# Block transposes of ten head pairs on VectorE: placed later, in quarters, each pair hashed by itself, value means per pair

## The chip, the cores and the metric

The kernel runs on one core of a Trainium2 chip. The metric is the device time of one execution in microseconds (us); lower is better. The engines are TensorE (PE in the profile; PEld is its weight loads), VectorE (DVE), ScalarE (ACT), GpSimd (POOL) and the queues that issue DMAs, above all SyncE's (SP). Each engine works through its own instructions in order; between engines there are semaphores.

## The reference

Attention in which a query sees only the keys of its own hash bucket, followed by a gated feed-forward block on the normalised result (4 batches, 8 heads, 768 tokens, 64 columns per head):

```python
    q_bits = (np.einsum('bhsd,dk->bhsk', q, proj) > 0).astype(np.int64)
...
    mask = q_bucket[:, :, :, None] == k_bucket[:, :, None, :]
    scores = np.where(mask, scale * np.matmul(q, k.transpose(0, 1, 3, 2)), -1000000000.0)
    attn = np.exp(scores - np.max(scores, axis=-1, keepdims=True))
    attn = attn / (np.sum(attn, axis=-1, keepdims=True) + 1e-09)
    x = np.matmul(attn, v)
...
    xn = x / np.sqrt(np.mean(x * x, axis=-1, keepdims=True) + 1e-06) * rms_g
    g = xn @ w_gate
    out = (g * (1.0 / (1.0 + np.exp(-g))) * (xn @ w_val)) @ w_out
```

## The kernel before, in words

**Units, slots and stages.** The work is cut into eight units u: half the queries (384) of a batch b = u // 2. A unit has eight heads, and a head three chunks of keys; so there are 192 chunks. The main loop at the end of the function has one *slot* t for each of them. In slot t the program issues the score matmuls of chunk t + 1 (`scores`, L337), the Exp of chunk t (`probs`, L349, on ACT), and then whatever the list `plan[t]` holds. The n-th Exp in the trace therefore marks slot n. 24 slots are a *stage*: stage w has slots 24w to 24w + 23. `at(w, s, f, ...)` puts a step into slot 24w + s, and steps of one slot are issued in the order in which they were put there.

**Regular steps.** `av` (L362) multiplies the probabilities of a head by the values, in two parts, into `o_ps`, of which there is one buffer for a pair of heads. After the second head of a pair comes `attn_out`: VectorE adds the mean of the values (`otmp`, L376, which reads `o_ps` and `cvb`), takes the reciprocal (L381), and POOL makes `x` (L383) and its square `sq` (L388). `sumsq` (L392, VectorE) sums the square some slots later. In slot 4 of stages 2 to 7 stands `norm` of the unit just finished: `ss` on VectorE (L402), `rstd` on POOL (L406), then three `xn` on VectorE (L409). Around slots 5 to 7 `turn_x` turns `xn` on TensorE (`x_ps`, L416) and VectorE writes it back (`xnT`, L422). Then `gate` and `value` run the feed-forward's first two products (L433): ACT takes a tanh (L441), VectorE makes `a` (L450) and `ht` (L451). `project` (L462) does the last product of the unit before, and `store` copies it out on ACT (L474) and sends it through SP (L475).

**Banks.** `d_ps` (hash), `m_ps` (value mean), `x_ps`, `g_ps`, `v_ps` and `y_ps` share three PSUM banks: a tile takes a bank that is free in program order and waits on the chip until its previous tenant has been read.

**Placing.** `spread` puts the 36 project matmuls, the turns of x and the 96 feed matmuls of a stage into its 24 slots by weights (in ns), so that each slot gets an equal share. The dictionary `hashes` (slot: weight, step) takes part in this: a hash takes its place ahead of a whole piece in its slot, and its weight pushes later pieces back.

**Pairs of heads.** q and k of a pair (b, hp) must be turned so that the 64 columns lie on partitions. Six pairs, (0, 0) to (0, 3), (1, 0) and (1, 1), are turned on TensorE. The other ten are loaded in blocks of 32 columns (`load_blocks`, L117, eight DMAs on SP; `load_v`, L103) and turned on VectorE (`turn_dve`, a 32x32 block transpose: L175 for batch 1, L181 for batches 2 and 3), k and q in two halves each. POOL casts the turned tiles to fp16 into `QK` (`cast_pool`, L194), and the values into `vl` (`v_prep`, L305); for batches 2 and 3 it also adds up values (`v_sum`, L311 to L313). `v_mean` (L321) sums values over the tokens on TensorE with a matrix of ones, and VectorE writes `cvb` (L324).

**Hashes.** `hash_one` multiplies k and q of a pair by the projection (L202, four matmuls into four row groups of one bank), takes signs (L210), spreads them into two head forms (`select`, L217, two instructions) and sends them by four DMAs on SP (L278) into rows 64 to 75 of `QK`, where `scores` reads them. `hash_two` does two pairs at once in two banks, with two sign instructions, two selects of double width and four DMAs (L297).

**Where things stand before.** The dictionary `spots` gives for each batch the slots of the loads and of the first half turn; the four halves go into four consecutive slots. Pairs (1, 2) and (1, 3) are hashed by `hash_one` in slots 52 and 60, the other eight by `hash_two` in slots 80, 93, 111 and 135. The block transposes end in slot 132.

Of the kernel before, what the change touches and what calls it, by code (L numbers as in the profile page):

```python
# [9 lines left out]
FP16 = mybir.dt.float16  # L10
# [6 lines left out]
S = 768  # L17
# [4 lines left out]
HALF = 384  # L22
# [9 lines left out]
def kernel(  # L32
# [12 lines left out]
    nc = tc.nc  # L45
# [10 lines left out]
    spool = ctx.enter_context(tc.tile_pool(name="spool", bufs=2))  # L56
# [24 lines left out]
    def bank(name, shape=None, dt=FP32):  # L81
        return gps.tile(shape or [128, 512], dt, name=name, tag="g")
# [47 lines left out]
    ONPE = [(0, hp) for hp in range(4)] + [(1, 0), (1, 1)]  # L130
    KROWS = D + 12
    KROWS0 = D + 6
    qT, kT, QK = {}, {}, {}
# [34 lines left out]
            turned(b, hp, which)[64 * e : 64 * e + 64, h0 : h0 + n, :],  # L168
        )

    def turn_dve(b, hp, which, part):
        src = raw[b, hp][0 if which == "q" else 1]
        dst = (qT if which == "q" else kT)[b, hp]
        if b in PARITY:
            nc.vector.transpose(  # L175
                dst.rearrange("p (e j t r) -> p e r j t", e=2, j=3, r=4)[:, part],
                src.rearrange("p (r j e) d -> p e r j d", j=3, e=2)[:, part],
            )
            return
        r = slice(2 * part, 2 * part + 2)  # L180
        nc.vector.transpose(  # L181
            dst.rearrange("p (c t r) -> p r c t", c=6, r=4)[:, r],
            src.rearrange("p (r c) d -> p r c d", r=4)[:, r],
        )
# [13 lines left out]
    def hash_half(parts):  # L198

        ps = bank("d_ps", [128, HALF])  # L200
        for t, src in parts:
            nc.tensor.matmul(  # L202
                ps[32 * t : 32 * t + 32, :], pj[:, 0:32], src,
                start=True, stop=True, tile_position=(0, 32 * t),
            )
        return ps

    def signs(bt, ps, c0, n):

        nc.vector.tensor_scalar(  # L210
            out=bt[0:n, 1, c0 : c0 + HALF], in0=ps[0:n], scalar1=0.0, scalar2=0.5,
            op0=ALU.is_gt, op1=ALU.subtract,
        )

    def select(bt, n, w):
        for hh in range(2):
            nc.vector.tensor_scalar_mul(  # L217
                bt[0:n, hh, 0:w], bt[0:n, 1, 0:w], sel[0:n, hh : hh + 1]
            )
# [15 lines left out]
    def hash_direct(b, hp, heads):  # L235


        where = [(which, hh) for which in "kq" for hh in heads]
        pss = hash_pairs([turned(b, hp, which)[:, hh, :] for which, hh in where])
        bt = spool.tile([128, 2, S], FP16, name="bits")  # L240

        def sign(e):
            signs(bt[:, :, e * HALF :], pss[e], 0, 32 * len(where))

        def move(e, kinds="kq", n=1, only=heads):
            for t, (which, hh) in enumerate(where):
                if which in kinds and hh in only:
                    o = (0 if which == "q" else S) + e * HALF
                    nc.vector.tensor_scalar_mul(
                        QK[b, 2 * hp + hh, "h"][64:KROWS0, o : o + n * HALF],  # L250
                        bt[32 * t : 32 * t + 6, 1, e * HALF : (e + n) * HALF],
                        4.0 * BIT * BIT if which == "k" else 1.0,
                    )

        def send():
            nc.vector.tensor_scalar_mul(bt[:, 0, :], bt[:, 1, :], own)
            for t, (which, hh) in enumerate(where):
                o = 0 if which == "q" else S
                nc.sync.dma_start(
                    out=QK[b, 2 * hp + hh, "h"][64:KROWS0, o : o + S],  # L260
                    in_=bt[32 * t : 32 * t + 6, 0, :],
                )

        return sign, move, send

    def hash_one(b, hp):
# [9 lines left out]
        for t, which, half in where:  # L276
# [2 lines left out]
                out=QK[b, hp][64:KROWS, :, o : o + HALF],  # L279
                in_=bt[32 * t : 32 * t + 12, :, 0:HALF],  # L280
            )

    def hash_two(b, hp):

        bt = spool.tile([128, 2, S], FP16, name="bits")
        for half in range(2):
            c0 = half * HALF
            ps = hash_half(
                [(2 * i + j, t[b, hp + i][:, c0 : c0 + HALF])
                 for i in range(2) for j, t in enumerate((kT, qT))]  # L290
            )
            signs(bt, ps, c0, 128)
        select(bt, 128, S)
        for i in range(2):
            for j, o in enumerate((S, 0)):
                p0 = 64 * i + 32 * j
                nc.sync.dma_start(  # L297
                    out=QK[b, hp + i][64:KROWS, :, o : o + S], in_=bt[p0 : p0 + 12]
                )


    def v_prep(b, hp):
# [204 lines left out]
    for t in range(4):  # L507
        p0 = 32 * t
# [36 lines left out]
    NS = 24  # L545
# [5 lines left out]
    def at(w, s, f, *a):  # L551
        plan[NS * w + s].append(lambda: f(*a))
# [7 lines left out]
    sign, move, _ = hash_direct(0, 0, (0,))  # L560
# [63 lines left out]
    for hp, ts in ((0, (8, 22, 23, 24, 25, 24, 26, 26, 28, 42)), (1, (12, 27, 28, 29, 30, 29, 41, 32, 33, 43))):  # L624
        tl, ts = ts[0], ts[1:]
        for w in "kq":
            at(0, tl, load_natural, nc.sync, 1, hp, w)
        at(0, tl, load_v, nc.sync, 1, hp)
        at(0, ts[0], new_pair, 1, hp)
        for t, hh, w in zip(ts[0:4], (0, 1, 0, 1), "kkqq"):  # L630
            at(0, t, turn_pe, 1, hp, hh, w)
        at(0, ts[4], cast_pool, 1, hp, "k")
        at(0, ts[5], cast_pool, 1, hp, "q")
        at(0, ts[6], hash_pair, 1, hp)
        at(0, ts[7], send_pair, 1, hp)
        at(0, ts[8], v_prep, 1, hp)
        at(2, 6 + 6 * hp, v_mean, 1, hp, 2, range(6))
    spots = {
# [3 lines left out]
    }  # L642
    sqs = {}

# [19 lines left out]

    SCORES, AV, PROJ, FEED, TURN = 330, 290, 216, 324, 220
    hashes = {t: (700, hash_one, 1, hp) for hp, t in ((2, 52), (3, 60))}
    for b, ts in ((2, (80, 93)), (3, (111, 135))):
        for i, t in enumerate(ts):  # L670
            hashes[t] = (1430, hash_two, b, 2 * i)

    def spread(t0, n, pieces):
        fixed = [SCORES + (AV if (t - 1) % 3 < 2 else 0) for t in range(t0, t0 + n)]
# [22 lines left out]
    for u in range(7):  # L697
# [11 lines left out]
        for i in range(9):  # L709
            c, n = divmod(i, 3)  # L710
# [9 lines left out]
    for t, (_, *step) in hashes.items():  # L720
        at(0, t, *step)

    for b, (loads, turns) in spots.items():
        for hp in range(4):
            if (b, hp) in ONPE:
                continue
            t = loads[hp]
            at(0, t, load_blocks, nc.sync, b, hp)
            at(0, t, load_v, nc.sync, b, hp)
            t = turns[hp]  # L730

            late = 5 if t % NS == 0 else 0
            at(0, t, new_pair, b, hp)
            at(0, t, turn_dve, b, hp, "k", 0)
            at(0, t + 1, turn_dve, b, hp, "k", 1)
            at(0, t + 2 + late, cast_pool, b, hp, "k")
            at(0, t + 2, turn_dve, b, hp, "q", 0)
            at(0, t + 3, turn_dve, b, hp, "q", 1)
            at(0, t + 4 + late, cast_pool, b, hp, "q")
            at(0, t + 5 + late, v_prep, b, hp)  # L740
            if b > 1:
                at(0, t + 5 + late, v_sum, b, hp)
                if hp % 2:
                    at(2 * b, 1 + hp, v_mean, b, hp - 1, 4)
            else:
                at(2 * b, 6 + 6 * hp, v_mean, b, hp, 2, range(6))


    def head_of(t):
# [61 lines left out]
```

## Time and profile before

| | us |
|---|---|
| three runs | 347.31, 347.76, 347.92; median 347.76 |
| the profiled execution | 348.43 |
| its span in the trace | 346.7 |

| engine | busy us | share of the span | instructions |
|---|---|---|---|
| PE | 330.3 | 95% | 3031 |
| DVE | 246.5 | 71% | 477 |
| ACT | 225.9 | 65% | 327 |
| POOL | 147.4 | 43% | 210 |

| group | line | count | mean ns |
|---|---|---|---|
| block transposes of k / q, batches 2 and 3 | L181 | 16 / 16 | 881 / 873 |
| block transposes of k / q, batch 1 | L175 | 4 / 4 | 892 / 865 |
| signs of a hash, 128x384 | L210 | 20 | 553 |
| select, 128x768 / 128x384 | L217 | 8 / 4 | 844 / 468 |
| cvb, 128x130 / 128x260 | L324 | 8 / 4 | 286 / 424 |
| a / ht | L450 / L451 | 96 / 96 | 550 / 554 |
| xn | L409 | 24 | 665 |

[...] The granted TensorE clock was 1.0 of full speed throughout. In the timeline a row is start, length, engine, line, operation, output<-inputs, shapes and count; in brackets stands the idle time of the engine just before it and the instruction that ended it.

### The profile page before, as it was taken

How to read it: one execution, taken by the hardware profiler on the slowest of the kernel's cores; microseconds unless marked ns; L12 is line 12 of the kernel's file. 1: busy time of each engine (PE TensorE's matmuls, PEld its weight loads, DVE VectorE, ACT ScalarE, POOL GpSimd, SP SyncE). 2: the span in 40 equal slices, each digit the busy share in tenths (PEclk: the TensorE clock that was granted, in tenths of full speed). 3: DMA queues.
4: the chain of work that ended last, by engine and by line, in shares of the span. 5: the costliest groups of instructions: out<-in, count | busy, mean ns of one | idle time of the engine just before them, and what ended most of it. 6: DMA issues, size and time to landing. Idle time of an engine off the chain costs nothing.

```text
span 346.7 us, 7724 instructions
## 1 busy us (share of the span) xinstructions
PE 330.3 (95%) x3031; PEld 199.5 (58%) x3031; DVE 246.5 (71%) x477; ACT 225.9 (65%) x327; POOL 147.4 (43%) x210
## 2 busy tenths in 40 slices
PE   8798988998989999999999999999999999999996
PEld 4465745654656655555565656565666656664554
DVE  3679966777898678998788677984566546674870
ACT  2789984666665756666577766768577776863322
POOL 4389956204558046863386144841111121112000
PEclk9999999999999999999999999999999999999999
DMA  7899938907557081782753010010100010001002
GB/s 243 284 203 294 220 91 147 172 2 140 143 102 137 2 174 63 128 156 50 145 121 76 12 61 32 3 17 3 62 30 2 2 61 32 0 3 61 33 0 93
DMA packets 78453, 31.21 MB, mean 90 GB/s; under 512 B 64736, under 2 KB 74448, under 8 KB 78416
## 3 DMA queue, kind: packets, MB, share of 16 engines
q1 hardware_dynamic: 75312, 25.73, 30.8%
q0 software_dynamic: 2656, 4.72, 7.8%
q8 instruction: 24, 0.39, 0.5%
q10 hardware_dynamic: 448, 0.27, 0.2%
q14 instruction: 13, 0.11, 0.1%
HBM read 28.32 MB, written 6.29 MB: 100 GB/s over the span
## 4 chain that ended last, share of the span: by engine, by line
PE 73%; DVE 14%; POOL 4%; issue 3%; DMA 3%; ACT 2%; SPq 0%; DVEq 0%; POOLq 0%
PE v_ps L433 16%; PE g_ps L433 15%; PE s_ps L337 13%; PE y_ps L462 12%; PE o_ps L362 8%; DVE xn L409 3%; PE t_ps L150 2%; PE d_ps L227 2%; DMA qL<-in_q_dram 2%; DVE otmp L376 1%; ACT psb L349 1%; PE z_ps L533 1%; POOL rstd L406 1%; DVE xnT L422 1%; DVE kT L181 1%
## 5 line engine op out<-in xcount | busy, mean ns | idle before, releaser
L349 ACT ACTIVATE psb<-s_ps,ebias 128x768 f16<-128x768 f32 x192 | 168.1, 900 | 31.5 <-PE s_ps L337 30.3
L337 PE MATMUL s_ps<-QK 76*128 76x384 f16 (+1 forms) x384 | 93.6, 325 | 3.9 <-ACT psb L349 1.3
L383 POOL TENSOR_TENSOR x<-otmp,rcp 128x384 f32<-128x384 f32 x32 | 26.5, 829 | 139.8 <-DVE rcp L381 139.3
L441 ACT ACTIVATE t<-g_ps 128x384 f32<-128x384 f32 x96 | 47.2, 492 | 57.6 <-PE g_ps L433 57.5
L433 PE MATMUL v_ps<-xnT,wv 128*128 128x384 f16 x384 | 81.6, 325 | 1.8 <-DVE a L450 1.7
L433 PE MATMUL g_ps<-xnT,wg 128*128 128x384 f16 x384 | 82.5, 325 | 0.1
L450 DVE SCALAR_TENSOR_TENSOR a<-t,g_ps 128x384 f32<-128x384 f32 x96 | 52.8, 550 | 26.7 <-ACT t L441 24.9
L462 PE MATMUL y_ps<-wo,ht 128*128 128x512 f16 x276 | 67.8, 378 | 0.0
L362 PEld LDWEIGHTS <-psb 128*128 128x128 f16 x1152 | 51.8, 97 | 20.6 <-issue 4.7
L451 DVE SCALAR_TENSOR_TENSOR ht<-a,v_ps 128x384 f16<-128x384 f32 x96 | 53.2, 554 | 11.2 <-PE v_ps L433 2.0
L362 PE MATMUL o_ps<-vl,psb 128*128 128x65 f16 x1152 | 56.4, 193 | 2.5 <-DVE otmp L376 2.5
L337 PEld LDWEIGHTS <-QK 76*128 76x128 f16 (+1 forms) x384 | 35.3, 98 | 33.6 <-issue 6.6
L433 PEld LDWEIGHTS <-wv 128*128 128x128 f16 x384 | 35.7, 97 | 25.0 <-issue 3.5
L433 PEld LDWEIGHTS <-wg 128*128 128x128 f16 x384 | 33.9, 97 | 20.1 <-DVE xnT L422 0.6
L462 PEld LDWEIGHTS <-ht 128*128 128x128 f16 x276 | 24.7, 97 | 22.6
L376 DVE TENSOR_TENSOR otmp<-o_ps,cvb 128x390 f32<-128x390 f32 x32 | 17.9, 560 | 15.3 <-PE o_ps L362 15.2
L388 POOL TENSOR_TENSOR sq<-x 128x384 f32<-128x384 f32 x32 | 26.4, 826 | 2.5
L474 ACT COPY ysb<-y_ps 128x512 f32<-128x512 f32 x23 | 13.5, 586 | 18.4 <-PE y_ps L462 18.3
L392 DVE TENSOR_REDUCE ssp<-sq 128x3 f32<-128x384 f32 x32 | 17.1, 535 | 7.5 <-POOL sq L388 7.4
L409 DVE TENSOR_SCALAR xn<-x,rstd 128x512 f16<-128x512 f32 x24 | 14.7, 665 | 7.8 <-POOL rstd L406 7.8
L422 DVE TENSOR_TENSOR xnT<-x_ps,gcol 128x512 f16<-128x512 f16 x23 | 14.9, 685 | 5.1 <-PE x_ps L416 5.1
L194 POOL CAST QK<-qT 64x768 f16<-64x768 f32 x20 | 16.4, 822 | 4.8 <-DVE qT L181 4.2
(74 smaller groups left out, 271.3 us busy)
## 6 DMA issues: line engine op xcount, KB each, us to landing
vn<-in_v_dram SPq DMA_DIRECT2D x16, 384.0 KB
out_dram<-ysb SPq DMA_DIRECT2D x23, 256.0 KB
qL<-in_q_dram SPq DMA_DIRECT2D x40, 96.0 KB
kL<-in_k_dram SPq DMA_DIRECT2D x40, 96.0 KB
kn<-in_k_dram SPq DMA_DIRECT2D x5, 384.0 KB
qn<-in_q_dram SPq DMA_DIRECT2D x5, 384.0 KB
wg<-in_moe_w_gate_dram POOLq DMA_DIRECT2D x2, 768.0 KB, 8.5
wv<-in_moe_w_val_dram POOLq DMA_DIRECT2D x2, 768.0 KB, 9.3
```

Source lines behind the costliest of these rows:

```text
L337: nc.tensor.matmul(ps[:, j, 0:HALF], QK[b, h, "h"][0:rows, S + jt * 128 : S + (jt + 1) * 128], QK[b, h, "h"][0:rows, half * HALF : (half + ...
L349: nc.scalar.activation(psb[u, h][:, 2 * ch : 2 * ch + 2, :], sps.pop((u, i))[:, :, 0:HALF], AF.Exp, bias=ebias, scale=ESCALE,)
L362: nc.tensor.matmul(o[:, c, hh, 0:65], psb[u, h][:, jt, c * 128 : (c + 1) * 128], vls[b % 2][:, h, 2 * (jt % 3) + jt // 3 if b in PARITY el ...
L376: nc.vector.tensor_add(tmp[:, :, :, 0:65], o[:, :, :, 0:65], cvb[b % 2][:, 2 * hp : 2 * hp + 2, 0:65].unsqueeze(1).to_broadcast([128, 3, 2 ...
L383: nc.gpsimd.tensor_mul(xd.rearrange("p c (h d) -> p c h d", h=2), tmp[:, :, :, 0:64], r.to_broadcast([128, 3, 2, 64]),)
L388: nc.gpsimd.tensor_mul(sq, xd, xd)
L409: nc.vector.tensor_scalar_mul(xn[u][:, c, :], x[u][:, c, :], rstd[:, c : c + 1])
L433: nc.tensor.matmul(ps, w[:, kt, fs], xnT[u][:, kt, :], start=(kt == 0), stop=(kt == 3))
L441: nc.scalar.activation(t, fbank[u, ft, "g_ps"], AF.Tanh, scale=0.5)
L450: nc.vector.scalar_tensor_tensor(out=a, in0=t, scalar=1.0, in1=g, op0=ALU.add, op1=ALU.mult)
L451: nc.vector.scalar_tensor_tensor(out=ht[u][:, ft, :], in0=a, scalar=0.5, in1=vv, op0=ALU.mult, op1=ALU.mult)
L462: nc.tensor.matmul(y, ht[u][:, ft, c * 128 : (c + 1) * 128], wo[:, ft, :], start=(ft == 0), stop=(ft == NF - 1),)
```

## The change

The loads, turns and hashes of the ten pairs get slots of their own, pair by pair. Pairs (1, 2) and (1, 3) are still turned in halves, the eight pairs of batches 2 and 3 in quarters, one in a slot for the most part, two in a slot in 96, 97, 99 and 105 and in 144, 145, 147 and 153. The last turn stands in slot 153. `hash_two` is gone: each pair has its `hash_one`, with a weight of 1000 in the placing (700 before; `hash_two` had 1430). Casts, `v_prep` and `v_sum` that would fall in slots 2 to 6 of a stage go to its slot 7. `v_mean` of batches 1 to 3 is done per pair in slots 3, 9, 15 and 21 of the batch's first stage; before, batch 1 had slots 6, 12, 18 and 24, and batches 2 and 3 two pairs at a time in slots 2 and 4. Because the hashes' places and weights change, `spread` moves some project, feed and x-turning pieces by a slot: the first turn of x goes from slot 77 to 78 in stage 3 and from 101 to 102 in stage 4.

```diff
-    def turn_dve(b, hp, which, part):
+    def turn_dve(b, hp, which, part, parts=4):
...
-        r = slice(2 * part, 2 * part + 2)
+        n = 4 // parts
+        r = slice(n * part, n * part + n)
...
-        at(2, 6 + 6 * hp, v_mean, 1, hp, 2, range(6))
+        at(2, 3 + 6 * hp, v_mean, 1, hp, 2, range(6))
     spots = {
-        1: ((None, None, 20, 45), (None, None, 48, 56)),
-        2: ((51, 59, 65, 76), (61, 72, 81, 87)),
-        3: ((84, 92, 100, 108), (96, 105, 120, 129)),
+        (1, 2): (20, (48, 49), (50, 51), 52),
+        (1, 3): (45, (57, 58), (59, 60), 61),
+        (2, 0): (52, (63, 64, 65, 66), (67, 69, 70, 71), 73),
+        (2, 1): (61, (72, 73, 75, 81), (82, 83, 84, 85), 86),
+        (2, 2): (70, (87, 88, 89, 90), (91, 93, 94, 95), 97),
+        (2, 3): (84, (96, 96, 97, 97), (99, 99, 105, 105), 106),
+        (3, 0): (93, (107, 108, 109, 111), (112, 113, 114, 115), 117),
+        (3, 1): (102, (120, 121, 123, 129), (130, 131, 132, 133), 134),
+        (3, 2): (114, (135, 136, 137, 139), (140, 141, 142, 143), 145),
+        (3, 3): (132, (144, 144, 145, 145), (147, 147, 153, 153), 154),
     }
...
-    SCORES, AV, PROJ, FEED, TURN = 330, 290, 216, 324, 220
+    SCORES, AV, PROJ, FEED, TURN, HASH = 330, 290, 216, 324, 220, 1000
-    hashes = {t: (700, hash_one, 1, hp) for hp, t in ((2, 52), (3, 60))}
-    for b, ts in ((2, (80, 93)), (3, (111, 135))):
-        for i, t in enumerate(ts):
-            hashes[t] = (1430, hash_two, b, 2 * i)
+    hashes = {spot[3]: (HASH, hash_one, *pair) for pair, spot in spots.items()}
...
-            late = 5 if t % NS == 0 else 0
-            at(0, t, turn_dve, b, hp, "k", 0)
-            at(0, t + 1, turn_dve, b, hp, "k", 1)
-            at(0, t + 2 + late, cast_pool, b, hp, "k")
-            at(0, t + 2, turn_dve, b, hp, "q", 0)
-            at(0, t + 3, turn_dve, b, hp, "q", 1)
-            at(0, t + 4 + late, cast_pool, b, hp, "q")
-            at(0, t + 5 + late, v_prep, b, hp)
-            if b > 1:
-                at(0, t + 5 + late, v_sum, b, hp)
-                if hp % 2:
-                    at(2 * b, 1 + hp, v_mean, b, hp - 1, 4)
-            else:
-                at(2 * b, 6 + 6 * hp, v_mean, b, hp, 2, range(6))
+    def behind_norm(t):
+        return t - t % NS + 7 if 2 <= t % NS < 7 else t
+    for (b, hp), (load, kturns, qturns, _) in spots.items():
+        at(0, load, load_blocks, nc.sync, b, hp)
+        at(0, load, load_v, nc.sync, b, hp)
+        at(0, kturns[0], new_pair, b, hp)
+        for w, turns in (("k", kturns), ("q", qturns)):
+            for i, t in enumerate(turns):
+                at(0, t, turn_dve, b, hp, w, i, len(turns))
+            at(0, behind_norm(turns[-1] + 1), cast_pool, b, hp, w)
+        t = behind_norm(qturns[-1] + 2)
+        at(0, t, v_prep, b, hp)
+        if b > 1:
+            at(0, t, v_sum, b, hp)
+            at(2 * b, 3 + 6 * hp, v_mean, b, hp, 2)
+        else:
+            at(2 * b, 3 + 6 * hp, v_mean, b, hp, 2, range(6))
```

More of the change, by code (lines that the diff above doesn't have):

```diff
@@ L281, in hash_one @@
             )
[L283 to L299, printed above, removed]
     def v_prep(b, hp):
@@ L721 @@
         at(0, t, *step)
[L723 to L730, printed above, removed]
-            late = 5 if t % NS == 0 else 0
-            at(0, t, new_pair, b, hp)
-            at(0, t, turn_dve, b, hp, "k", 0)
-            at(0, t + 1, turn_dve, b, hp, "k", 1)
-            at(0, t + 2 + late, cast_pool, b, hp, "k")
-            at(0, t + 2, turn_dve, b, hp, "q", 0)
-            at(0, t + 3, turn_dve, b, hp, "q", 1)
-            at(0, t + 4 + late, cast_pool, b, hp, "q")
-            at(0, t + 5 + late, v_prep, b, hp)
-            if b > 1:
-                at(0, t + 5 + late, v_sum, b, hp)
-                if hp % 2:
-                    at(2 * b, 1 + hp, v_mean, b, hp - 1, 4)
-            else:
-                at(2 * b, 6 + 6 * hp, v_mean, b, hp, 2, range(6))
+    def behind_norm(t):
[15 more added lines that the diff above has]
+            at(2 * b, 3 + 6 * hp, v_mean, b, hp, 2, range(6))
     def head_of(t):
```

## The prediction

> **What bounds the kernel now.** I read the page first, then the busy times by stage, the waits of TensorE, and the timeline around each wait. Part 4 of the page:
>
> ```profile
> PE 73%; DVE 14%; POOL 4%; issue 3%; DMA 3%; ACT 2%; SPq 0%; DVEq 0%; POOLq 0%
> ```
>
> TensorE carries the chain that ends last; whatever does not make TensorE work or wait is free. The change lies in slots 48 to 167. Cut at the starts of Exps 48, 72, 96, 120, 144 and 168, the busy times are (columns: stretch, length, then busy time and instructions of PE, PEld, DVE, ACT, POOL, granted clock, DMA):
>
> ```profile
> 74.00:116.00 42.00, 39.84 (x372) 23.96 (x371) 34.16 (x64) 27.49 (x41) 21.57 (x27) 1.00 0.53 108
> 116.00:158.20 42.20, 40.55 (x376) 23.54 (x374) 35.63 (x64) 27.39 (x40) 25.08 (x33) 1.00 0.54 107
> 158.20:197.70 39.50, 38.87 (x356) 23.20 (x355) 31.23 (x57) 27.37 (x40) 19.66 (x26) 1.00 0.44 89
> 197.70:236.90 39.20, 38.56 (x354) 22.92 (x353) 30.69 (x55) 27.31 (x40) 19.41 (x25) 1.00 0.08 26
> 236.90:273.80 36.90, 36.83 (x340) 22.92 (x339) 22.33 (x45) 27.24 (x40) 7.48 (x9) 1.00 0.06 22
> ```
>
> These are stages 2 to 6. Stage 6 turns and hashes nothing and takes 36.9 us; the others take 2.3 to 5.3 us more. Part of that is work (hashes, value means), part is TensorE's idle time: 2.16, 1.65, 0.63, 0.64 and 0.07 us, 5.15 in all. Who ended it, in slots 48 to 144 (columns: waiter, releaser, us in total, times, longest):
>
> ```profile
> PE v_ps L433 <- DVE a L450: 1.7, 3, 0.8
> PE x_ps L416 <- DVE xn L409: 1.3, 3, 0.5
> PE m_ps L321 <- DVE bits L210: 1.1, 1, 1.1
> ```
>
> Always VectorE. A score matmul's record lasts 0.326 us, but a pair takes 0.49, so the next can start after 0.163; a gap of x therefore loses about x + 0.16. From start to start I count, per stage: 2.9 (m_ps at 85.7: 1.30; d_ps at 96.2: 0.39; v_ps at 103.3: 0.94; small 0.29), 2.45 (x_ps 0.97, v_ps 1.48), 1.28 (x_ps 1.11), 1.13 (x_ps 0.96) and 0: **7.8 us, the most that better placing can return**.
>
> Two timeline rows show why x_ps waits (start, length, instruction):
>
> ```profile
> 125.02 1.78 POOL L194 CAST QK<-kT 64x768 f16<-64x768 f32 x2
> 125.08 2.39 DVE L409 TENSOR_SCALAR xn<-x,rstd 128x512 f16<-128x512 f32 x3 [0.97 <-POOL rstd L406]
> ...
> 244.85 1.28 DVE L409 TENSOR_SCALAR xn<-x,rstd 128x512 f16<-128x512 f32 x3 [0.97 <-POOL rstd L406]
> ```
>
> With casts on POOL behind rstd, the three xn take 2.39 us; without, 1.28. The first xn, which x_ps waits for, takes 1.03 instead of 0.48.
>
> **The change, part by part.**
>
> *Quarter turns.* The eight pairs of batches 2 and 3 take 64 quarters for 32 halves. Two halves in a row take 1.57, so one occupies VectorE for 0.71. A quarter costs at least 0.36 (no fixed part) and at most 0.45 (a fixed part of 0.19, a whole reciprocal of six elements, L381). I take 0.39 (a fixed part of 0.06, the 128x1 memset of L517, nearer to an issue cost): 25.0 us for 22.7, hidden unless VectorE is the late one. [...]
>
> *VectorE by stage.* With base rows unchanged, halves 0.71, quarters 0.39, hash_one about 1.55 (sign 0.55, two selects 0.7 to 1.27), hash_two 2.8 (two signs, two selects of 0.84), cvb 0.29: stage 2 loses 4 halves and gains 8 quarters and small things, 34.2 to 34.8; stage 3 35.6 to 30.7; stage 4 31.2 to 33.9; stage 5 30.7 to 29.9; stage 6 22.3 to 28.8. The load is levelled, not cut.
>
> *Hashes.* Eight d_ps records occupy TensorE from 80.96 to 81.74 = 0.78 (0.79 at slot 60), sixteen from 223.16 to 224.59 = 1.43. Before: 2 x 0.79 + 4 x 1.43 = 7.3; after: 10 x 0.79 = 7.9. **+0.6 us**, on the path. SP's DMAs for them go from 24 to 40 (0.85 each to issue); SP has room, but they stand behind loads and before stores there.
>
> *Value means.* Batches 2 and 3 take eight matmuls of 130 columns (0.06 start to start) for four of 260 (0.11): 0. Their banks now come out of the feed stretch, at slots 9, 15, 21 of stages 4 and 6; a bank is held until cvb has read it (0.39 lost at 96.15 in such a place).
>
> *Loss after, stage 2: 2.65.* The first mean is ahead of the norm, but hash (1,2) still takes its bank across it; x_ps inherits that bank and the wait. Behind rstd POOL now runs all four casts and v_prep of pair (1,2) at once (4.2 us instead of 1.78), so the third xn also takes about 1.03: the bank comes free 0.55 later, TensorE arrives 0.39 later (one mean moved ahead): 1.30 becomes 1.65. Hash (1,3) stands right behind a half turn: 0.4; feed 0.6 of 1.2, as slots 61 and 62 turn nothing.
>
> *Stage 3: 0.8.* The k cast of (2,1) moves to slot 82, so xn is free (first xn 0.55 sooner), and hash (2,0) at slot 73 gives TensorE 0.79 ahead of x_ps. Against that, slots 72 and 73 now hold a q cast, v_prep and v_sum on POOL (1.7 + 0.82 + 0.99 + 0.46 + 0.46 = 4.4 us) in front of attn_out's x. Counted from the start of slot 72: POOL is free at 6.2, rcp done at 6.2, sq 7.9, rstd 9.6, first xn 10.2; TensorE reaches x_ps at 10.3. x_ps 0.2, hash behind its turn at slot 86 0.2, feed 0.4 of 1.48.
>
> *Stage 4: 1.7.* The same crowd, and six quarters in slots 96 to 99 with sign and selects between: otmp of the last pair starts about 6.3 us into the stage. o_ps has one buffer, whose next matmuls stand at 6.5: 0.4 lost. The k cast of (2,3) still follows rstd, so xn stays slow: x_ps 0.75. Hash behind two quarters at slot 106 0.15, feed 0.4.
>
> *Stage 5: 0.2.* No cast behind rstd any more; first xn 0.55 sooner against a wait of 0.65.
>
> *Stage 6: 0.65.* New: a cast behind rstd, the crowd in front of it. TensorE has 0.79 more work ahead; x_ps 0.2, hash 154 behind two quarters 0.3, feed 0.15.
>
> **The sum.** Loss 7.8 to 6.0 = -1.8; hashes +0.6: **-1.2 us**. The profiled execution took 348.43 (span 346.7, 1.7 around it), so 347.2; the shown runs have a median of 347.76, and 347.76 - 1.2 = **346.6 us**.
>
> **Rivals.**
>
> *All stalls that quarters can reach go.* For it: feed stalls came behind 0.71 us turns, and VectorE has 8 us unused in stage 3. Then only the opening of stage 2 (1.65) and about 1.4 of slow xn stay: loss 3.1, -4.7 + 0.6 = -4.1: 343.7. Chance 0.17.
>
> *The crowd in front of the norms decides; slower.* At slots 73, 97 and 145 two selects fall into POOL's run of casts and adds. One such pair took 1.27 at 97.72 where POOL was busy, against 0.68 at 85.69 where it was idle. If each select waits out an add (0.35 + 0.9, twice: 2.5), otmp starts 1.2 later in three stages. It costs from the point where otmp of the fourth pair starts later than the next o_ps matmuls could, 6.5 us into stages 3, 4 and 6; then almost all of it: 3 x 1.0 = +3.0: 349.6. Against it: the 1.27 itself. [...] Chance 0.20.
>
> *The loss follows VectorE's load, not its grain.* Before, 81, 84, 79, 78 and 60% busy went with 2.9, 2.45, 1.28, 1.13 and 0 lost. After, 82, 79, 84, 79 and 74% would lose 2.7, 1.25, 2.5, 1.2 and 0.7 = 8.35: +0.55 + 0.6: 348.9. Chance 0.10.
>
> *Hash (1,3) lands late.* It goes from slot 60 to 61, its first reader stays the score matmul issued in slot 65. Before, 7.3 us lay between; one slot (1.6) less is 5.7, and sign, selects, two of four DMAs (1.75 to issue) and about 1 us to land take about 5. If it is late by 1 us: 347.6. Chance 0.08.
>
> *A quarter is dear* (0.45, and more where it waits): 64 x 0.06 = 4 us more VectorE work, in feed slots that have little to spare: per three slots (4.75 us) 2.3 tiles of feed at 1.13 (L450 and L451, start to start), attn_out 0.77 and sumsq 0.45 leave 0.9, 0.3 a slot. VectorE then bounds the feed: some 350 to 353. Chance 0.05.
>
> **Chances.** The forecast, 345.3 to 347.4, has 0.40. What a measurement of this kernel tells from no change is about 0.2%, 0.7 us. Faster by more: 0.33 of the forecast, the first rival 0.17, late hash 0.02: 0.52. Within: 0.07 + 0.06 + some of the crowd and load cases 0.05: 0.18. Slower: 0.30. The range of 8 in 10 is 343.6 to 349.4.
>
> **What would show it.** Right: three xn in 1.28 in stages 3 and 5 and 2.39 or more in 2, 4 and 6; stage 3 shorter by about 3 us, stage 5 by more than 1, stage 6 longer by about 2; no idle PE behind `a` over 0.5. Wrong: PE o_ps waiting for otmp in three stages, score matmuls waiting for QK's landing near slot 65, quarters over 0.6 us long, or stage 2 shorter than before by over 1 us.

## The result and the profile after

| | us |
|---|---|
| before, 14 runs | 347.77 median (346.96 to 350.02) |
| after, 14 runs | 346.43 median (345.76 to 348.41) |
| after / before | 0.9962, 95% interval 0.9945 to 0.998 |
| the profiled execution of after, and its span | 346.98, 345.2 |

The changed kernel is faster by 1.3 us (0.7 to 1.9 by the interval); 346.6 was forecast. Part 4 of its page shows TensorE with still more of the chain that ends last, 80% for 73%:

```profile
PE 80%; DVE 9%; POOL 4%; issue 4%; ACT 2%; DVEq 0%; POOLq 0%
```

The busy times of stages 2 to 6, cut at the same Exps as before (length, then PE, PEld, DVE, ACT, POOL, granted clock, DMA):

```profile
74.10:115.90 41.80, 40.25 (x378) 24.18 (x377) 34.64 (x68) 27.34 (x41) 17.52 (x21) 1.00 0.44 89
115.90:154.40 38.50, 38.49 (x354) 22.67 (x352) 30.07 (x65) 27.32 (x41) 19.43 (x25) 1.00 0.49 101
154.40:195.00 40.60, 39.69 (x366) 23.18 (x364) 34.29 (x73) 27.50 (x41) 22.33 (x29) 1.00 0.42 89
195.00:232.70 37.70, 37.69 (x346) 22.64 (x344) 28.38 (x61) 27.15 (x40) 16.57 (x22) 1.00 0.25 58
232.70:272.50 39.80, 39.17 (x358) 23.00 (x357) 30.19 (x62) 27.38 (x40) 17.85 (x23) 1.00 0.07 25
```

Length less PE is TensorE's idle time. Stage by stage the lengths move by -0.2, -3.7, +1.1, -1.5 and +2.9 us, -1.4 together. TensorE's busy time grows by 0.6, from 194.7 to 195.3, and its idle time falls from 5.15 to 3.1. Stages 3 and 5 have none left (0.01 each); what remains lies in stages 2, 4 and 6: 1.55, 0.91 and 0.63. The waits of TensorE in this stretch (waiter, releaser, us in total, times, longest) say where:

```profile
PE x_ps L400 <- DVE bits L212: 1.4, 1, 1.4
PE x_ps L400 <- DVE xn L393: 1.3, 2, 0.9
PE m_ps L305 <- DVE a L434: 0.2, 1, 0.2
PE v_ps L417 <- DVE a L434: 0.2, 1, 0.2
```

The waits of `v_ps` behind `a`, 1.7 us in three places before, are down to one of 0.2. The wait for a hash's signs has only changed its owner: it was the value mean's, now the first turn of x waits for that bank. The wait for `xn` happens twice, in stages 4 and 6, where it was three times, in stages 3, 4 and 5.

The timeline shows the reason: VectorE's `xn` and POOL's casts in stages 2 to 6 (start, length, instruction).

```profile
82.88 2.96 DVE L393 TENSOR_SCALAR xn<-x,rstd 128x512 f16<-128x512 f32 x3 [0.99 <-POOL rstd L390]
85.76 0.54 DVE L212 TENSOR_SCALAR bits<-d_ps 128x384 f16<-128x384 f32 x1
...
125.84 1.28 DVE L393 TENSOR_SCALAR xn<-x,rstd 128x512 f16<-128x512 f32 x3 [0.97 <-POOL rstd L390]
...
164.88 1.78 POOL L196 CAST QK<-kT 64x768 f16<-64x768 f32 x2
164.96 2.38 DVE L393 TENSOR_SCALAR xn<-x,rstd 128x512 f16<-128x512 f32 x3 [0.97 <-POOL rstd L390]
...
242.68 2.38 DVE L393 TENSOR_SCALAR xn<-x,rstd 128x512 f16<-128x512 f32 x3 [0.97 <-POOL rstd L390]
```

In stage 3 (and in 5) the three `xn` take 1.28; in 4 and 6, where a pair of casts runs beside them, 2.38; in stage 2, where four casts do (82.81 to 86.52), 2.96, and only then does the sign come that frees the bank.

### The profile page after: what moved, and what is told of

It reads as the page before. It is cut to its first block, busy times and chain, and to the rows that moved or that the text cites. A ratio compares the mean times of both kernels' runs of the same rounds, so it can differ in the third digit from the quotient of the medians.

```text
span 345.2 us, 7819 instructions
## 1 busy us (share of the span) xinstructions
PE 331.2 (96%) x3035; PEld 198.6 (58%) x3035; DVE 249.8 (72%) x521; ACT 225.7 (65%) x327; POOL 147.8 (43%) x210
## 4 chain that ended last, share of the span: by engine, by line
PE 80%; DVE 9%; POOL 4%; issue 4%; ACT 2%; DVEq 0%; POOLq 0%
PE v_ps L417 17%; PE g_ps L417 17%; PE s_ps L321 15%; PE y_ps L446 13%; PE o_ps L346 9%; PE t_ps L150 2%; PE d_ps L204 2%; PE d_ps L229 2%; PE x_ps L400 2%; DVE xn L393 2%; PE z_ps L517 1%; ACT psb L333 1%; DVE bits L212 1%; POOL rstd L390 1%; POOL x L367 1%
## 5 line engine op out<-in xcount | busy, mean ns | idle before, releaser
L321 PEld LDWEIGHTS <-QK 76*128 76x128 f16 (+1 forms) x384 | 34.3, 98 | 34.9 <-issue 9.3
L417 PEld LDWEIGHTS <-wg 128*128 128x128 f16 x384 | 34.7, 97 | 21.1 <-DVE xnT L406 0.6
L196 POOL CAST QK<-kT 64x768 f16<-64x768 f32 x20 | 16.7, 833 | 13.9 <-DVE kT L183 9.2
```

Source lines behind the costliest of these rows:

```text
L196: nc.gpsimd.tensor_copy(QK[b, 2 * hp + hh, "h"][0:64, o : o + S], src[64 * hh : 64 * hh + 64, :])
L321: nc.tensor.matmul(ps[:, j, 0:HALF], QK[b, h, "h"][0:rows, S + jt * 128 : S + (jt + 1) * 128], QK[b, h, "h"][0:rows, half * HALF : (half + ...
L417: nc.tensor.matmul(ps, w[:, kt, fs], xnT[u][:, kt, :], start=(kt == 0), stop=(kt == 3))
```

## The experiments

Each was timed in five rounds against the kernel before. Two theories stood. **Norm**: the change works through what POOL does around a norm (a cast behind `rstd`, sums in front of the last `x`), and through the bank that a hash holds across it. **Grain**: shorter turns, and hashes one by one, let VectorE serve the feed sooner. "Start to start" is the time by which TensorE's next instruction starts later than in an undisturbed run of the same kind.

**halves.** The changed kernel, each pair turned in halves, in the slots of its second and fourth quarter.

```diff
+    spots = {
+        p: (l, k if len(k) == 2 else k[1::2], q if len(q) == 2 else q[1::2], h)
+        for p, (l, k, q, h) in spots.items()
+    }
```

> The changed kernel with halves instead of quarters for the eight pairs of batches 2 and 3: a half stands where the second and the fourth quarter stood; all else is the same. Norm theory (the change pays through what stands around rstd and in front of x_ps, not through the grain of the turns): within 0.4 us of the changed kernel, 346.0 to 346.9, because two quarters in a row take 0.87 (0.36 each) and a half 0.71, so VectorE's work is the same. Grain theory (quarters keep a and ht in time): at least 1.5 us slower, 348 or more, with waits of v_ps or g_ps for a (L434) of 1.5 us in all in stages 2 to 6 again, where the changed kernel has 0.2.

Measured: 347.25, ratio 0.9981 (0.9965 to 0.9997). The waits of `v_ps` do not come back:

```profile
PE o_ps L346 <- DVE otmp L360: 0.3, 1, 0.3
PE m_ps L305 <- DVE a L434: 0.2, 1, 0.2
PE v_ps L417 <- DVE a L434: 0.2, 1, 0.2
```

So they did not go because the turns are shorter. In the kernel before, a half turn or two stand right in front of the two `a` that TensorE waits for longest (turns from 101.98 and from 137.57); the change moves these turns, and with them the hashes and some feed pieces, and no run parts the two. The interval overlaps with that of the change; by the medians the quarters are worth 0.8 us, and `o_ps` (0.45 start to start in stage 4, 0.20 with quarters) is one place where.

**hash1.** The kernel before, with ten single hashes and nothing else of the change; the slots of the batches 2 and 3 are my own choice.

```diff
-    for b, ts in ((2, (80, 93)), (3, (111, 135))):
+    for b, ts in ((2, (66, 80, 86, 93)), (3, (104, 111, 128, 135))):
         for i, t in enumerate(ts):
-            hashes[t] = (1430, hash_two, b, 2 * i)
+            hashes[t] = (700, hash_one, b, i)
```

> The kernel before with hash_one for each pair (slots 66, 80, 86, 93, 104, 111, 128 and 135 for the pairs of batches 2 and 3, weight 700), turns in halves where they were, means where they were. Per-pair theory (single hashes bring the gain, because two signs and two wide selects no longer stand in front of a): about 1 us faster than before, v_ps waits in stage 3 gone. Norm theory: within 0.6 us of before; TensorE does 0.6 to 0.9 us more for the hashes, the v_ps waits of stage 3 (1.1 us behind the double hashes) shrink, and the x_ps waits of stages 3, 4 and 5 stay at about 0.7 each, since casts still stand behind rstd there.

Measured: 351.53, ratio 1.0101 (1.0074 to 1.0129), some 3 us slower than either theory expected. A hash now waits for its own half turn, and the feed waits oftener:

```profile
PE v_ps L433 <- DVE a L450: 2.2, 5, 0.7
...
PE d_ps L202 <- DVE qT L175: 0.5, 1, 0.5
```

These two add 1.0 to the waits of before. Stages 2 to 6 grew by 4.1 us. Counted from start to start, the feed's waits cost 1.9 more than before (13 of them for 8), the hash that waits for its turn 0.7 more, and the hashes' own matmuls 0.6; the rest is not placed. Since the slots are new too, it shows that single hashes are no gain by themselves, and nothing more.

**castlate.** The changed kernel, the k casts of (2, 3) and (3, 3) two slots later, in slot 9 of stages 4 and 6.

```diff
-            at(0, behind_norm(turns[-1] + 1), cast_pool, b, hp, w)
+            late = 2 if w == "k" and hp == 3 and b > 1 else 0
+            at(0, behind_norm(turns[-1] + 1) + late, cast_pool, b, hp, w)
```

> The changed kernel with the k casts of pairs (2,3) and (3,3) in slots 105 and 153 instead of 103 and 151, that is behind x and sq of slots 104 and 152 in POOL's order and no longer straight behind rstd. Norm theory: the three xn of stages 4 and 6 take 1.28 us instead of 2.38, the first one 0.48 instead of 1.03; x_ps waits 0.45 instead of 1.03 in stage 4 and 0 instead of 0.57 in stage 6: 1.1 us faster than the changed kernel, about 345.3. Rival (xn's length is covered, the chain is late already at otmp; or the casts only hit something else later): no change within 0.3 us.

Measured: 345.45, ratio 0.9927 (0.9902 to 0.9952). The wait for `xn`, start to start, goes from 1.03 to 0.49 in stage 4 and from 0.57 to 0 in stage 6, as the norm theory had it. The norm of stage 4:

```profile
164.82 1.28 DVE L393 TENSOR_SCALAR xn<-x,rstd 128x512 f16<-128x512 f32 x3 [0.97 <-POOL rstd L390]
```

**signfirst.** The changed kernel; the sign of hash (1, 2) goes ahead of the first `xn` of stage 2, its selects and DMAs behind the third.

```diff
     def norm(u, signs_of=None):
...
+        rest = hash_start(*signs_of) if signs_of else None
...
+        if rest:
+            rest()
```

> The changed kernel with the sign of hash (1,2) issued on VectorE between ss and xn of the norm in slot 52, instead of behind the three xn; its selects and DMAs still come behind xn, and the hash matmuls stand where they stood. Bank theory (x_ps waits 1.5 us in stage 2 because it inherits the bank of this hash, which is free only when its sign, behind three slow xn, has read it): the sign fits into VectorE's idle time of about 1 us while POOL makes rstd, the bank is free before xn, x_ps waits about 0.1, and the kernel is 1.0 to 1.4 us faster than the changed one, about 345.2. Rival (x_ps waits for xn anyway, and the next parts for xnT behind the selects): under 0.4 us faster.

Measured: 346.26, ratio 0.9956 (0.9941 to 0.9972): no different from the change. The bank is free in time (the sign is done at 82.42, as `xn` starts), but now the selects stand between `xn` and `xnT`, for which the third turn waits:

```profile
82.40 2.96 DVE L401 TENSOR_SCALAR xn<-x,rstd 128x512 f16<-128x512 f32 x3
85.28 1.76 DVE L219 TENSOR_SCALAR bits<-bits,sel 128x384 f16<-128x384 f16 x2
86.96 1.87 DVE L416 TENSOR_TENSOR xnT<-x_ps,gcol 128x512 f16<-128x512 f16 x3
```

```profile
PE x_ps L410 <- DVE xnT L416: 1.3, 1, 1.3
PE s_ps L328 <- DMA QK<-bits: 0.3, 1, 0.3
```

The wait for the signs (1.4) became one for `xnT` (1.3): VectorE has the same work to do before the third turn, so the wait moved to the next instruction in line and did not go. The second wait (0.48 start to start) is that of the score matmul of slot 65 for hash (1, 3). That hash was sent no later than in the changed kernel (its first DMA is issued 26.9 us into the stage, there 27.0), yet it landed too late in this execution; why is not shown.

**oldcasts.** The kernel before, with one line changed: the casts and sums of the pairs turned from slots 72, 96 and 120 stand two slots later, the k cast in slot 9 of its stage instead of 7.

```diff
-            late = 5 if t % NS == 0 else 0
+            late = (5 if b == 1 else 7) if t % NS == 0 else 0
```

> The kernel before with one number changed: of the pairs turned at the start of stages 3, 4 and 5, the k cast goes to slot 9 of the stage instead of 7 (q cast 11, v_prep and v_sum 12), so that no cast stands straight behind rstd there; stage 2 stays. Norm theory: xn takes 1.28 us instead of 2.39 in three stages, x_ps waits of 0.97, 1.11 and 0.96 us shrink by 0.5 to 0.6 each: 1.6 us faster than before, about 346.2, that is as much as the whole change. Rival (the whole change is needed, since turns and double hashes behind the norm hold VectorE): under 0.6 us faster.

Measured: 344.53, ratio 0.9898 (0.987 to 0.9926). One line is worth 3.4 us by the medians (2.6 to 4.5 by the interval, 2.8 in the stages of the trace), more than the whole change and about twice what the norm theory expected. In stage 4 `xn` is back at 1.28, and of the waits of before only these are left of any size:

```profile
166.14 1.28 DVE L409 TENSOR_SCALAR xn<-x,rstd 128x512 f16<-128x512 f32 x3 [0.97 <-POOL rstd L406]
```

```profile
PE v_ps L433 <- DVE a L450: 1.7, 3, 0.8
PE m_ps L321 <- DVE bits L210: 1.1, 1, 1.1
```

I had expected half of each `x_ps` wait to go, by the first `xn` alone (0.55). The whole wait goes in all three stages (0.97, 1.11 and 0.96 become 0.13, 0 and 0). The later two `xn` come sooner too: the third ends 1.1 sooner, and with it comes everything behind it on VectorE, so that the later turns of x lose their waits as well.

**casts35.** The changed kernel, with two casts of a junk tile on POOL behind `rstd` in stages 3 and 5, where the change had left none.

```diff
+    def more_casts(u):
+        for _ in range(2):
+            nc.gpsimd.tensor_copy(junk, x[u][0:64, :, 0:256])
+    at(0, 79, more_casts, 2)
+    at(0, 127, more_casts, 4)
```

> The changed kernel with work added: two more POOL casts (64x768, fp32 to fp16, of x into an unused tile) straight behind rstd in stages 3 and 5, where the changed kernel has none. Norm theory: the three xn there take 2.38 us instead of 1.28, x_ps waits 0.6 to 0.7 in stage 3 (0.14 now) and 0.5 to 0.7 in stage 5 (0 now): 1.0 to 1.2 us slower than the changed kernel, about 347.6. Rival: these two stages have slack there, under 0.3 us.

Measured: 347.65, ratio 0.9992 (0.9972 to 1.0013): 1.2 us above the change, nearly all of its gain. The same norm as at 125.84 above, now with a cast in front of it, and the waits:

```profile
124.99 1.78 POOL L737 CAST junk<-x 64x768 f16<-64x768 f32 x2
```

```profile
125.06 2.38 DVE L393 TENSOR_SCALAR xn<-x,rstd 128x512 f16<-128x512 f32 x3 [0.97 <-POOL rstd L390]
```

```profile
PE x_ps L400 <- DVE xn L393: 2.3, 4, 0.9
```

Two casts that nobody reads stretch `xn` from 1.28 to 2.38, and TensorE waits for it four times instead of twice.

**old35.** The other way round: the kernel before, with only the norms of stages 3 and 5 cleared (the q casts and sums of these two pairs move by two slots with the k casts).

```diff
-            late = 5 if t % NS == 0 else 0
+            late = (7 if t in (72, 120) else 5) if t % NS == 0 else 0
```

> The kernel before with the casts, v_prep and v_sum of the pairs turned from slots 72 and 120 two slots later, so that no cast stands straight behind rstd in stages 3 and 5: the same two norms that the change clears, and nothing else of the change. If clearing these two norms is the change's whole gain, and all else in it (quarters, places of the turns, single hashes, means) comes out at nothing in sum: as fast as the changed kernel or up to 0.5 us faster, 345.8 to 346.4 (x_ps waits of 0.97 and 0.96 us gone). If the rest of the change gives something of its own: clearly slower than the changed kernel, 347 or more.

Measured: 346.58, ratio 0.9956 (0.9935 to 0.9977), the same as the whole change (0.9962). Stage 4's wait stays, split in parts, and so do those for `a` (1.7) and for the signs (1.1).

**turnlate.** The changed kernel, the second pair of quarters in slots 97 and 145 one slot later.

```diff
-        (2, 3): (84, (96, 96, 97, 97), (99, 99, 105, 105), 106),
+        (2, 3): (84, (96, 96, 98, 98), (99, 99, 105, 105), 106),
...
-        (3, 3): (132, (144, 144, 145, 145), (147, 147, 153, 153), 154),
+        (3, 3): (132, (144, 144, 146, 146), (147, 147, 153, 153), 154),
```

> The changed kernel with the two quarters of slots 97 and 145 moved to slots 98 and 146, where they stand behind attn_out instead of in front of it. In the changed kernel otmp of stage 4 starts at 160.62, 1.9 us after its matmuls, straight behind these two quarters (0.72 us). If VectorE's queue in front of otmp sets when rstd comes, the 0.2 us wait of o_ps in stage 4 goes, x_ps waits 0.3 to 0.5 instead of 1.03 there, and the kernel is 0.6 to 0.9 us faster; in stage 6, where x starts when POOL is done with v_sum (239.18), nothing changes. If POOL's run of cast, v_prep and v_sum sets it in stage 4 too (done at 160.92), the gain is 0.4 at most.

Measured: 345.7, ratio 0.9932 (0.9909 to 0.9954), 0.7 below the change, as expected. `otmp` of the last pair in stage 4 no longer stands behind those quarters, and starts 5.54 us into the stage instead of 6.27 (the stage's first Exp is at 154.35 in the changed kernel and at 154.03 in this one). First the changed kernel, then this one:

```profile
159.89 0.87 DVE L183 STREAM_TRANSPOSE kT<-kL 128x192 f32<-128x192 f32 x2
160.62 0.53 DVE L360 TENSOR_TENSOR otmp<-o_ps,cvb 128x390 f32<-128x390 f32 x1
```

```profile
159.57 0.55 DVE L360 TENSOR_TENSOR otmp<-o_ps,cvb 128x390 f32<-128x390 f32 x1
```

The wait of `o_ps` (0.20) is gone, and `x_ps` in stage 4 falls from 1.03 to 0.65. Stage 6 keeps its 0.57.

**vlate.** The changed kernel; `v_prep` and `v_sum` of slots 73, 97 and 145 come eight slots later.

```diff
         t = behind_norm(qturns[-1] + 2)
+        t += 8 if t % NS == 1 else 0
```

> The changed kernel with v_prep and v_sum of slots 73, 97 and 145 eight slots later, in slot 9 of the stage, so that POOL runs one q cast and not 4.5 us of work in front of x of the norm's last pair. Crowd theory (POOL's run in front of attn_out sets rstd, and slows the selects in VectorE's queue): in stage 6 x no longer starts behind v_sum, in stage 4 the selects take 0.35 each instead of 0.65; rstd comes 0.4 to 0.8 us earlier, x_ps waits 0 to 0.2 instead of 0.57 in stage 6 and 0.5 instead of 1.03 in stage 4: 0.6 to 1.1 us faster than the changed kernel. Rival (VectorE's own turns in front of otmp set it): under 0.3 us.

Measured: 344.87, ratio 0.991 (0.9884 to 0.9936), 1.6 below the change and more than expected. In stage 6 POOL now waits for the last pair's reciprocal, and starts its `x` 5.69 us into the stage; in the changed kernel it stood behind the sums and started at 6.48 (first Exps at 231.32 and 232.70). First the changed kernel, then this one:

```profile
239.18 0.83 POOL L367 TENSOR_TENSOR x<-otmp,rcp 128x384 f32<-128x384 f32 x1
```

```profile
237.01 0.83 POOL L367 TENSOR_TENSOR x<-otmp,rcp 128x384 f32<-128x384 f32 x1 [2.13 <-DVE rcp L365]
```

The `x_ps` wait falls to 0.67 in stage 4 and to 0 in stage 6, `o_ps` waits no more. In stage 4 the two selects, now without `v_prep` and the sums beside them, take 0.68 together (at 157.81) instead of 1.29, and `otmp` starts 0.63 sooner. The crowd in front of the norms, which the prediction had as a rival, is real.

**open2.** The changed kernel; the whole hash (1, 2) goes between `rstd` and `xn` of stage 2, and the q cast and `v_prep` of that pair to slot 57.

```diff
     def norm(u, signs_of=None):
...
+        if signs_of:
+            hash_one(*signs_of)
...
-        t = behind_norm(qturns[-1] + 2)
+            late = 2 if (b, hp, w) == (1, 2, "q") else 0
+        t = behind_norm(qturns[-1] + 2) + (2 if (b, hp) == (1, 2) else 0)
```

> The changed kernel with sign and both selects of hash (1,2) ahead of xn in the norm of slot 52, and with q cast and v_prep of this pair in slot 57 instead of 55 (behind x and sq of slot 56). After the kernel with the sign alone ahead of xn, where the wait of 1.5 us only moved from the first turn of x to the third, which waits for xnT behind the selects (1.42): if the opening of stage 2 is bound by VectorE's sum of xn, sign, selects and xnT, taking 0.55 us from the third xn and the selects out from between leaves a wait of 0.3 to 0.8 and gives 0.7 to 1.2 us. Risk: score matmuls of slot 59 wait for the q cast, up to 0.5. Rival (the time is set by feed's start for another reason): under 0.3 us.

Measured: 345.18, ratio 0.9913 (0.9885 to 0.9941), 1.25 below the change, as expected. The 1.52 lost at the first turn of x becomes 0.23: the selects, ahead of `xn` now, take 1.70, and the three `xn` behind them are short again, 1.26 for 2.96.

```profile
83.83 1.70 DVE L219 TENSOR_SCALAR bits<-bits,sel 128x384 f16<-128x384 f16 x2
85.45 1.26 DVE L395 TENSOR_SCALAR xn<-x,rstd 128x512 f16<-128x512 f32 x3
```

**best2.** The changed kernel with castlate, turnlate and open2 together.

> The changed kernel with three edits that helped one by one: k casts of (2,3) and (3,3) in slots 105 and 153; two quarters each from slots 97 and 145 to 98 and 146; sign and selects of hash (1,2) ahead of xn, with its q cast and v_prep in slot 57. Measured singly against before: 0.9927, 0.9932 and 0.9913, the changed kernel 0.9962. If the three remove different waits, the ratio is near 0.9962 - 0.0035 - 0.002 - 0.0049 = 0.986 (the first two share the 1.03 us wait of stage 4): about 343.0, with no wait of x_ps over 0.2 left in stages 2 to 6.

Measured: 343.52, ratio 0.9871 (0.9841 to 0.9901). It beats both kernels. Stages 2 to 6 hold 195.6 us for 195.1 of TensorE's work, and these are the waits that the trace still names:

```profile
PE m_ps L305 <- POOL sq L372: 0.2, 1, 0.2
PE v_ps L419 <- DVE a L436: 0.2, 1, 0.2
```

**oldbest.** The kernel before with the same care and none of the change's turns and hashes: oldcasts, hash (1, 2) ahead of `xn`, and the first two means of batch 1 in slots 51 and 60.

```diff
-        at(2, 6 + 6 * hp, v_mean, 1, hp, 2, range(6))
+        at(2, 3 if hp == 0 else 12, v_mean, 1, hp, 2, range(6))
...
-    hashes = {t: (700, hash_one, 1, hp) for hp, t in ((2, 52), (3, 60))}
+    hashes = {52: (700, lambda *a: None), 60: (700, hash_one, 1, 3)}
...
-            late = 5 if t % NS == 0 else 0
+            late = (5 if b == 1 else 7) if t % NS == 0 else 0
```

> The kernel before with its halves and double hashes, the late casts in stages 3, 4 and 5 (344.5 by themselves), sign and selects of hash (1,2) ahead of xn, and the means of (1,0) and (1,1) in slots 51 and 60. The 1.30 us wait of m_ps in stage 2 goes: about 343.3. What then still stands are waits for a behind half turns (0.95 at slot 65, 0.92 and 0.35 in stage 3). Against the changed kernel with all norm edits it shows what quarters and spread turns are worth once the norms are clear: if those waits are real losses, this kernel is 1 to 2 us slower than that one; if they only shift slack, within 0.5.

Measured: 344.04, ratio 0.9885 (0.9859 to 0.9911). The waits for `a` stay:

```profile
PE v_ps L435 <- DVE a L452: 1.7, 3, 0.8
```

It lies 0.5 us above best2, and the two intervals overlap. Best2 has lost these waits and pays 0.6 for its single hashes; the rest of the difference lies in pauses too short to be listed. What quarters, spread turns and single hashes are worth once the norms are clear is thus half a microsecond by the medians, and its sign is not settled.

## Why the prediction was right, and where its steps were off

The time (346.43 for 346.6) and the way it comes about were right. Clearing two norms in the kernel before gives the change's time (old35), and filling the same two in the changed kernel takes nearly all of it back (casts35). The rest of the change therefore sums to about nothing, though its parts are not small.

The intervals of castlate, turnlate and casts35 overlap with that of the change, but the lengths of the stages (us, from the starts of the Exps) settle it. In stages 3 to 6 of these runs only the stages whose norms were touched move by more than 0.03:

| stage | 3 | 4 | 5 | 6 |
|---|---|---|---|---|
| before | 42.25 | 39.48 | 39.23 | 36.91 |
| oldcasts (3, 4, 5 cleared) | 41.35 | 38.38 | 38.39 | 36.90 |
| old35 (3, 5 cleared) | 41.33 | 39.49 | 38.40 | 36.91 |
| after | 38.48 | 40.61 | 37.74 | 39.84 |
| castlate (4, 6 cleared) | 38.48 | 40.05 | 37.74 | 39.28 |
| casts35 (3, 5 filled) | 39.05 | 40.60 | 38.58 | 39.84 |
| turnlate (4, 6 touched) | 38.49 | 40.02 | 37.74 | 39.82 |

By the count from start to start:

| TensorE, us | before | after | predicted after |
|---|---|---|---|
| norms of stages 3 and 5 | 1.93 | 0.14 | 0.4 |
| norms of stages 4 and 6, `o_ps` with them | 1.11 | 1.80 | 1.35 |
| opening of stage 2 | 1.30 | 1.52 | 1.65 |
| feed, hashes' waits, banks | 3.44 | 1.56 | 2.6 |
| hashes' own matmuls | 7.4 | 7.9 | 7.9 (from 7.3) |

- **Norms of stages 3 and 5**: right, and the signs named beforehand are there: `xn` in 1.28 in these two and 2.38 or more in 2, 4 and 6, stage 3 shorter by 3.7 (about 3 foreseen), stage 5 by 1.5 (over 1), stage 6 longer by 2.9 (about 2).
- **Price of a cast beside xn**: it is not one number. The prediction took the first `xn` alone, 0.55 a norm. The stages of castlate (0.56 twice) and stage 3 of casts35 (0.57) bear that out; stage 5 of casts35 (0.84) and the kernel before (0.90, 1.10 and 0.84 in oldcasts) cost more, because there the second or third turn of x waited too.
- **Stages 4 and 6**: `x_ps` 1.03 and 0.57 instead of 0.75 and 0.2, `o_ps` 0.20 instead of 0.4. The cast behind `rstd` is part of it (castlate), the sums on POOL in front (vlate), in stage 4 also the quarters (turnlate).
- **Feed and hash waits**: over-estimated, 2.6 against 1.56. The feed and the hashes' waits thus gave as much (1.9) as the two cleared norms (1.8), more than twice the 0.84 foreseen. Hardly any hash waited behind its turn, although I had put 0.15 to 0.4 on four of them. The feed's waits went even with halves, so the shorter turns did not do it; that the places of the turns did is likely, and not parted from the places of the hashes.
- **Hashes**: +0.56 for +0.6. Ten times eight records, 0.79 each.
- **Quarter**: 0.39 was assumed and 0.36 measured, the lower bound: two in a row take 0.87, one alone 0.51. The row of the k quarters in the changed kernel (busy time, mean ns of one, idle time before):

```profile
L183 DVE STREAM_TRANSPOSE kT<-kL 128x192 f32<-128x192 f32 x32 | 15.8, 514 | 0.0
```

  No fixed part shows: 0.36 is half of a half's 0.71.
- **What the sum missed.** The terms of the table give -2.2, the time fell by 1.3. TensorE's busy and idle times close (+0.6 and -2.05, -1.4 in the stages), so the difference lies in pauses below the 0.12 us from which I counted. The near hit in time is partly errors that cancel: less loss in the feed, more at the norms and in small pauses.

**The rivals.** That the loss follows VectorE's load is false: stage 3 is busy to 78% and loses 0.3, stage 6 to 76% and loses 1.3. All stalls going (343.7) did not happen in the change, but best2 reaches it by other means. The crowd's mechanism is there (vlate), its price was smaller: the selects that fell among POOL's casts and sums in stages 4 and 6 took 1.29 and 1.12 a pair, near the 1.27 that spoke against it, not 2.5. In stage 6 the crowd also worked in a way the rival did not name: POOL's own `x` stood behind the sums. A hash landing late (0.48) showed only in signfirst. Dear quarters are out.

## What to carry to other kernels

Placing a step later in an engine's program order did not by itself make it run later here; what put it off was an instruction in front of it that waited itself. Slot 7 looked like "after the norm", but POOL had nothing else queued between slot 4 and slot 8, so the cast ran the moment `rstd` was done (at 125.02 in the kernel before, where `rstd` runs from 124.19 for 0.86); in slot 9 it stood behind an `x` that waits (in stage 6 of castlate POOL starts `rstd` at 241.09 and, after 4.78 idle, `x` at 246.72), and one line gave some 3 us (oldcasts). Look for what runs beside the few instructions on the path, on engines that seem free too, before moving work about to level a load; and when a wait ends, see which instruction on the same engine is next in line, for that is where it went in signfirst (1.4 behind the signs became 1.3 behind `xnT`).

## What the runs showed of the hardware

- `xn` (VectorE, fp32 from SBUF to fp16 in SBUF, 128x512) takes 0.48 alone and 1.03 beside a POOL cast; a select of 128x384 takes 0.32 alone and, where POOL worked beside it in the changed kernel, anything from 0.32 to 0.94. The casts lose little: a pair takes 1.78 instead of 1.70. `ht` and `a`, which read PSUM, keep their 0.55 (0.55 and 0.54 on average beside casts in the changed kernel). `xn` became 0.55 longer beside casts of 0.81 to 0.92 each, so a whole cast waited out is not what these lengths show.
- A block transpose has no fixed part that can be seen: in a row 128x384 comes every 0.71 us (two take 1.57, one 0.87), 128x192 every 0.36 (two take 0.87, one 0.51).
